# A hand-written step list that reaches from the start to the third batch's attention, in a kernel of cosine attention and a GELU feed-forward layer

## The chip, the cores and the metric

The kernel runs on one core of a Trainium2 chip. The metric is the device time of one execution in microseconds (us). TensorE does the matrix products, ScalarE the exponentials, the GELU and some squares, VectorE copies, sums and reciprocals, GpSimd the scaling of q and k and some squares and sums, and SyncE (SP) issues loads, stores and DMA transposes. GpSimd issues the loads that turn f32 into bf16. In the profile these engines are PE (and PEld for its weight loads), ACT, DVE, POOL and SP.

## The reference, cut to what matters

There are 8 batches, 12 heads, 448 positions and a head size of 64.

```python
q_n = q / (norm(q, axis=-1) + 1e-6);  k_n = k / (norm(k, axis=-1) + 1e-6)
scores = matmul(q_n, k_n.T) / tau                      # tau = 0.1
attn = exp(scores - max);  attn = attn / (sum(attn) + 1e-9)
x = matmul(attn, v)          # heads side by side: 3584 x 768
h = x @ w_in                 # 768 x 2048
g = 0.5 * h * (1 + erf(h / sqrt(2)))
out = g @ w_out              # 2048 x 768
```

## The kernel before

**Units of work.** Four heads of a batch make a quad g; a batch has three, so batch 0 has quads 0 to 2, batch 1 quads 3 to 5, batch 2 quads 6 to 8. The code also counts units u: quad 0 is cut into units 0 and 1, and from there unit u is quad u - 1. A quad's attention has these steps:

- `load_qk(g)` (L126) loads q and k through SP into one of four buffers, which is free again when the quad that held it has been scaled. `load_v` (L141), `load_wi` (L436) and `load_wo` (L445) are issued by POOL. `load_wo(0)` and `load_wo(1)` bring the upper and lower half of w_out's first 384 columns, `load_wo(2)` and `load_wo(3)` those of the last 384.
- `square`, `reduce`, `logs`, `roots`, `inverses`, `scale` (L151 to L208) give the normalised q and k in bf16: squares on ACT (L158) or POOL (L160), row sums on DVE (L168), Ln and Exp on ACT (L175, L180), the reciprocal on DVE (L188), the product on POOL (L204).
- `transposes` (L210) turns them, with TensorE and a DVE copy (`copies`, L226) up to unit 4, with a DMA on SP (L216) from unit 5.
- `scores` and `exps` (L232, L246) handle a quad in seven chunks: four matmuls into a pair of PSUM banks, then one Exp of 128x896 to SBUF. `visit(p)` (L654) does both for the next chunk in pair p. There are two pairs at first, and a third when batch 0's banks have been given up.
- The sum over keys is taken in three ways: `sums` (L298) with TensorE, `folded` (L258) with six POOL additions, `gathered` (L265) with DVE into PSUM. `turned` and `inverted`, or `turned_all` and `inverted_all` for the last two ways, bring the sums into place and invert them on DVE; `spread` (L362) lays them out.
- `values` (L324) multiplies by v, and `normalise` (L367) applies the inverse sum and writes x. It frees the banks that `values` filled.

**The feed-forward part.** x times w_in is the tile `hp` (`w_in`, L467): 16 column blocks m with six matmuls each. Each block is taken through GELU on ACT (L929). g times w_out is the tile `op` (`second_pieces`, L397): sixteen matmuls, called pieces, fill one of two banks, then a DVE copy (L410) empties it and SP stores it. Batch 0 gives 96 pieces and batch 1 128; the pieces are strewn between the scores of the next batch as filler for TensorE.

**What sets the order.** Each engine runs its instructions in the order of the program text, and each tile has a fixed buffer; an instruction waits for its data and for its buffer. Batch 0's attention is written out as a list (`attention_first`, L472). After it come `first(0)` (batch 0's hp), `attention(1)` (L702, pieces of batch 0, scores of batches 1 and 2), `first(1)`, `attention(2)`, `first(2)` and so on, each built by loops and counts such as

```python
        if b == 1:
            parts = iter((20, 13, 14, 17, 16, 16))
        elif b == 2:
            parts = iter((22, 12, 12, 13, 11, 13, 11, 11, 11, 6, 6))
```

which are the numbers of pieces between visits. `spin` (L460) issues idle matmuls. `total` (L371) for quads 3 to 7 uses `sums` on TensorE; quad 8 uses `folded`.

Of the kernel before, what the change touches and what calls it, by code (L numbers as in the profile page):

```python
# [9 lines left out]
F32 = mybir.dt.float32  # L10
# [6 lines left out]
def kernel(  # L17
# [108 lines left out]
    def load_qk(g):  # L126
        b, n = divmod(g, NQ)
        t = qkp.tile([128, 2, 2, C, D], F32, tag="qk", name=f"qk{g}")
        qk_t[g] = t
        for s0, s1 in ((0, 1), (1, 2)) if g == 0 else ((0, 2),):  # L130
            for i, src in enumerate((q, k)):
                eng = nc.scalar if g == 0 and s0 == 0 and i == 1 else nc.sync
# [131 lines left out]

    def gathered(g, p):  # L265
# [58 lines left out]
    def values(g, chunks=range(C), p=None):  # L324
        for c in chunks:
            if c == 0 and g < NQ:
# [70 lines left out]
    def second_pieces(sb, t, ni):  # L397
        state = {}

        def mm(kf):  # L400
# [8 lines left out]
            if kf == KF - 1:  # L409
                nc.vector.tensor_copy(ot[:, ni * NH:(ni + 1) * NH], ps[:, :NH])  # L410
# [7 lines left out]
        return [lambda kf=kf: mm(kf) for kf in range(KF)]  # L418
# [46 lines left out]
    early = {}  # L465

# [5 lines left out]
    def attention_first():  # L472
        x_t[0] = xp.tile([128, KD, S], BF16, tag="x", name="x0")
        DV, AC, GP = nc.vector, nc.scalar, nc.gpsimd
        Q, K = 0, 1
        square(0, ((AC, Q),))
        square(0, ((AC, K),))
        reduce(0, Q)
        reduce(0, K)
        square(1, ((AC, Q),))  # L480
        upto(load_v, 1)
        logs(0)
        reduce(1, Q)
        roots(0)
        upto(load_wi, 1)
        square(1, ((AC, K),))
        inverses(0)
        square(2, ((AC, Q),))
        reduce(1, K)
        scale(0, ((GP, 1),))  # L490
        logs(1)
        reduce(2, Q)
        roots(1)
        scale(0, ((GP, 0),))
        spin(2)
        transposes(0, 1)
        square(2, ((AC, K),))
        inverses(1)
        spin(1)
        transposes(0, 0)  # L500
        square(3, ((AC, Q),))
        copies(0, 1)
        scale(1, ((GP, 0),))
        copies(0, 0)
        square(3, ((AC, K),))
        scale(1, ((GP, 1),))
        upto(load_qk, 5)
        spin(1)
        transposes(1, 0)
        reduce(2, K)  # L510
        scores(0, ((0, 0), (0, 1)))
        upto(load_v, 2)
        transposes(1, 1)
        copies(1, 0)
        logs(2)
        scores(0, ((0, 2), (0, 3)))
        roots(2)
        upto(load_wi, 2)
        exps(0, ((0, 0), (0, 1)))
        inverses(2)  # L520
        copies(1, 1)
        exps(0, ((0, 2), (0, 3)))
        spin(2)
        scores(0, ((0, 4), (0, 5)))
        scale(2, ((GP, 0),))
        reduce(3, Q)
        exps(0, ((0, 4), (0, 5)))
        spin(1)
        scores(0, ((1, 0), (1, 1)))
        reduce(3, K)  # L530
        exps(0, ((1, 0), (1, 1)))
        spin(1)
        scores(0, ((1, 2), (1, 3)))
        scale(2, ((GP, 1),))
        upto(load_qk, 6)
        transposes(2, 0)
        exps(0, ((1, 2), (1, 3)))
        sums(0, (0,))
        copies(2, 0)
        scores(0, ((1, 4), (1, 5)))  # L540
        logs(3)
        scores(0, ((0, 6), (1, 6)))
        roots(3)
        transposes(2, 1)
        exps(0, ((1, 4), (1, 5)))
        inverses(3)
        sums(0, (1,))
        scale(3, ((GP, 0),))
        copies(2, 1)
        sums(0, (2,))  # L550
        exps(0, ((0, 6), (1, 6)))
        sums(0, range(3, 5))
        scores(1, ((0, 0), (1, 0)))
        scores(1, ((0, 1), (1, 1)))
        sums(0, (5,))
        exps(1, ((0, 0), (1, 0)))
        sums(0, (6,))
        upto(load_wi, 3)
        transposes(3, 0)
        turned(0)  # L560
        exps(1, ((0, 1), (1, 1)))
        scores(1, ((0, 2), (1, 2)))
        values(0, (0,))
        scale(3, ((GP, 1),))
        upto(load_wi, 4)
        copies(3, 0)
        values(0, (1,))
        exps(1, ((0, 2), (1, 2)))
        values(0, (2,))
        scores(1, ((0, 3), (1, 3)))  # L570
        inverted(0)
        values(0, range(3, 5))
        spread(0, 1)
        values(0, (5,))
        exps(1, ((0, 3), (1, 3)))
        scores(1, ((0, 4), (1, 4)))
        values(0, (6,))
        spread(0, 0)
        sums(1, (0,))
        square(4, ((GP, K),))  # L580
        exps(1, ((0, 4), (1, 4)))
        sums(1, (1,))
        scores(1, ((0, 5), (1, 5)))
        normalise(0, 0)
        transposes(3, 1)
        exps(1, ((0, 5), (1, 5)))
        scores(1, ((0, 6), (1, 6)))
        copies(3, 1)
        sums(1, (2,))
        square(4, ((GP, Q),))  # L590
        square(5)
        upto(load_wo, 2)
        exps(1, ((0, 6), (1, 6)))
        sums(1, range(3, 5))
        normalise(0, 1)
        scores(2, ((0, 0), (1, 0)))
        sums(1, (5,))
        exps(2, ((0, 0), (1, 0)))
        sums(1, (6,))
        scores(2, ((0, 1), (1, 1)))  # L600
        turned(1)
        values(1, range(2))
        exps(2, ((0, 1), (1, 1)))
        values(1, (2,))
        scores(2, ((0, 2), (1, 2)))
        inverted(1)
        values(1, range(3, 5))
        spread(1, 0)
        values(1, (5,))
        exps(2, ((0, 2), (1, 2)))  # L610
        values(1, (6,))
        scores(2, ((0, 3), (1, 3)))
        sums(2, (0,))
        reduce(4, K)
        normalise(1, 0)
        exps(2, ((0, 3), (1, 3)))
        sums(2, (1,))
        scores(2, ((0, 4), (1, 4)))
        spread(1, 1)
        values(2, (0,))  # L620
        sums(2, (2,))
        exps(2, ((0, 4), (1, 4)))
        scores(2, ((0, 5), (1, 5)))
        normalise(1, 1)
        values(2, range(1, 3))
        exps(2, ((0, 5), (1, 5)))
        values(2, (3,))
        scores(2, ((0, 6), (1, 6)))
        exps(2, ((0, 6), (1, 6)))
        reduce(4, Q)  # L630
        spin(1)
        early[4] = mm_tile("hp0_4")[:, :S]
        w_in(0, early[4], 4, range(2))
        sums(2, range(3, 7))
        values(2, (4,))
        logs(4)
        turned(2)
        values(2, (5,))
        roots(4)
        values(2, (6,))  # L640
        inverted(2)
        inverses(4)
        scale(4)
        spread(2, 1)
        spread(2, 0)
        normalise(2, 1)
        normalise(2, 0)
        done.update({square: 6, reduce: 5, root: 5, scale: 5, transposes: 5})

# [49 lines left out]

    def attention(b, fill):  # L702
        fill = list(fill)
        if b == 1:
            parts = iter((20, 13, 14, 17, 16, 16))
        elif b == 2:
            parts = iter((22, 12, 12, 13, 11, 13, 11, 11, 11, 6, 6))
        elif len(fill) == 128:
# [31 lines left out]
        if b == 1:  # L740
            upto(scale, u + 3)
            upto(load_v, b + 2)
            upto(transposes, u + 3)
            upto(load_qk, g0 + NQ + 2)
            upto(square, u + 4)
            visit(0, 1, 2)
            run()
            visit(0, 1, 2)
            run()
            upto(load_qk, g0 + NQ + 3)  # L750
            visit(0, 1)
            upto(square, u + 5)
            run()
            visit(0, 1, 2)
            both(g0, 0)
            upto(load_v, b + 3)
            upto(load_qk, g0 + NQ + 4)
            visit(1, 2)
            upto(reduce, u + 4)
            run()  # L760
            visit(1, 2, 0)
            both(g0 + 1, 1)
            visit(2, 0)
            logs(6)
            roots(6)
            run()
            both(g0 + 2, 2)
            inverses(6)
            done[root] = 7
        elif b == 2:  # L770
            upto(scale, u + 3)
            upto(load_qk, g0 + 6)
            upto(transposes, u + 3)
            upto(scale, u + 4)
            upto(load_qk, g0 + 7)
            upto(transposes, u + 4)
            visit(0, 1, 2)
            run()
            visit(0, 1, 2)
            norms(9)  # L780
# [230 lines left out]
```

## Time and profile before

| what | value |
|---|---|
| three runs | 400.55, 400.91, 400.94 us, median 400.91 |
| profiled execution, first to last instruction (span) | 398.6 us |
| around the span, median minus span | 2.3 us |
| busy PE, ACT, DVE, POOL | 392.0, 267.8, 264.0, 250.6 us |
| first hp matmuls of batch 0 that run on without a break | from 32.65 us |
| batch 0's hp ends, pieces and batch 1's scores begin | 51.33 us |
| batch 1's hp | 79.15 to 97.44 us |
| batch 2's hp begins | 133.45 us |

The page of the profile lists no separate device time for the profiled execution, so its own time is taken as its span and the 2.3 us around it. A row of the chain of waits has a start, a length in us, an engine, a tile and a line; x and a number count merged instructions. A row of a group has the line, engine, operation, result and operands, shapes, count, busy time in us, mean time of one in ns, and then the idle time ahead of it with what ended it. The profile counts a busy PE where matmuls overlap, so how full PE is is better read from the chain.

### The profile page before, as it was taken

To read this page: it belongs to the slowest core of one execution; us is meant where nothing else is said; L and a number is where in the kernel's file an instruction comes from. 1 tells how busy PE (TensorE), PEld (TensorE's weight loads), DVE (VectorE), ACT (ScalarE), POOL (GpSimd) and SP (SyncE) were. 2 spreads that over 40 slices of the span, in tenths; PEclk is the share of its full clock that TensorE was granted. 3 is DMA by queue.
4 is the path that set the end of the run, shared out by engine and by line. 5 is a ranking of instruction groups with operands and counts; after the bars stand their busy time and mean duration, and the time that the engine had idled before them with its cause. 6 is when DMAs were issued, how large, how long until landed. Compare 5 with 4: busy or idle time off the path is not lost.

```text
span 398.6 us, 8027 instructions
## 1 busy us (share of the span) xinstructions
PE 392.0 (98%) x3245; PEld 207.8 (52%) x3245; DVE 264.0 (66%) x530; ACT 267.8 (67%) x399; POOL 250.6 (63%) x162
## 2 busy tenths in 40 slices
PE   7999999999999999999999999999999999999996
PEld 3444555555545555555555555555555555555564
DVE  5787214955487999589963999769973797461021
ACT  6995787557988877888665977889656756504300
POOL 5898814269699694959587394969768391920000
PEclk9999999999999999999999999999999999999999
DMA  8999999747296890678145591566024720130033
GB/s 290 261 258 217 205 233 308 154 106 226 50 254 234 158 230 2 178 150 207 70 105 138 126 240 38 162 113 147 2 27 101 148 46 2 41 77 3 1 80 80
DMA packets 66485, 54.52 MB, mean 137 GB/s; under 512 B 38672, under 2 KB 62352, under 8 KB 66448
## 3 DMA queue, kind: packets, MB, share of 16 engines
q1 hardware_dynamic: 54464, 41.79, 39.0%
q0 software_dynamic: 11600, 11.80, 18.8%
q8 instruction: 25, 0.41, 0.4%
q10 hardware_dynamic: 384, 0.43, 0.3%
q14 instruction: 12, 0.10, 0.1%
HBM read 45.61 MB, written 11.01 MB: 142 GB/s over the span
## 4 chain that ended last, share of the span: by engine, by line
PE 95%; issue 1%; DVE 1%; POOL 1%; ACT 0%; POOLq 0%
PE hp L469 37%; PE op L406 36%; PE st L242 9%; PE o L320 4%; PE o L335 4%; PE op L425 1%; PE sm L305 1%; PE sh L667 1%; PE tp L221 1%; PE sm L314 1%; PE spin L463 0%; POOL wi L441 0%; DVE nq L168 0%; POOL qkb L204 0%; POOL v L145 0%
## 5 line engine op out<-in xcount | busy, mean ns | idle before, releaser
L252 ACT ACTIVATE pt<-st 128x896 bf16<-128x896 f32 x155 | 132.5, 916 | 29.0 <-PE st L242 28.4
L406 PE MATMUL op<-wo,g 128*128 128x384 bf16 x864 | 148.1, 326 | 0.0
L469 PE MATMUL hp<-x,wi 128*128 128x448 bf16 x768 | 147.0, 353 | 0.1
L204 POOL TENSOR_TENSOR qkb<-qk,rn 128x896 bf16<-128x896 f32 (+1 forms) x50 | 80.2, 1628 | 66.3 <-DVE rn L188 64.9
L406 PEld LDWEIGHTS <-g 128*128 128x128 bf16 x864 | 81.4, 98 | 62.6 <-issue 11.2
L469 PEld LDWEIGHTS <-wi 128*128 128x128 bf16 x768 | 74.4, 98 | 71.1 <-issue 2.8
L263 POOL TENSOR_TENSOR acc<-acc,pt 128x896 f32<-128x896 f32 x55 | 103.8, 1887 | 4.3
L929 ACT ACTIVATE g<-hp 128x448 bf16<-128x448 f32 x128 | 63.6, 552 | 63.6 <-PE hp L469 63.5
L410 DVE COPY ot<-op 128x384 f32<-128x384 f32 x54 | 29.9, 555 | 83.1 <-PE op L406 80.8
L168 DVE TENSOR_REDUCE nq<-sq 128x14 f32<-128x896 f32 (+1 forms) x50 | 50.6, 1038 | 10.2 <-POOL sq L160 6.7
L242 PE MATMUL st<-qkT 64*64 64x448 bf16 x620 | 46.0, 356 | 0.2 <-ACT pt L252 0.2
L160 POOL TENSOR_TENSOR sq<-qk 128x896 f32<-128x896 f32 x18 | 29.9, 1683 | 16.3 <-DMA qk<-in_q_dram 10.9
L369 DVE TENSOR_TENSOR x<-o,rs 128x448 bf16<-128x448 f32 x48 | 28.0, 609 | 9.9 <-PE sh L667 6.4
L270 DVE TENSOR_TENSOR acc<-acc,pt 128x896 f32<-128x896 f32 x30 | 33.0, 1099 | 1.0
L158 ACT ACTIVATE sq<-qk 128x896 f32<-128x896 f32 (+1 forms) x32 | 27.8, 902 | 2.2 <-DMA qk<-in_q_dram 1.8
L364 DVE STREAM_TRANSPOSE rs<-rc 128x448 f32<-128x448 f32 x48 | 28.7, 626 | 0.6
L242 PEld LDWEIGHTS <-qkT 64*64 64x64 bf16 x620 | 17.9, 105 | 20.5 <-issue 12.7
L263 POOL TENSOR_TENSOR acc<-pt 128x896 f32<-128x896 bf16 x11 | 20.7, 1879 | 8.9 <-DVE x L369 8.9
L320 PE MATMUL o<-pt,v 64*64 64x448 bf16 x364 | 24.2, 351 | 0.0
L673 ACT ACTIVATE pt<-sh 128x448 bf16<-128x448 f32 x26 | 14.1, 544 | 9.2 <-PE sh L667 8.5
L276 DVE STREAM_TRANSPOSE ta<-acc 128x448 f32<-128x448 f32 x32 | 18.5, 617 | 0.2
L335 PE MATMUL o<-pt,v 64*64 64x448 bf16 x308 | 17.5, 351 | 0.5 <-DVE x L369 0.5
(54 smaller groups left out, 212.4 us busy)
## 6 DMA issues: line engine op xcount, KB each, us to landing
qk<-in_q_dram SPq DMA_DIRECT2D x23, 448.0 KB, 4.6
qk<-in_k_dram SPq DMA_DIRECT2D x23, 448.0 KB, 5.4
out_dram<-ot SPq DMA_DIRECT2D x48, 192.0 KB, 3.2
v<-in_v_dram POOLq DMA_DIRECT2D x7, 672.0 KB, 7.7
wo<-in_moe_w_out_dram POOLq DMA_DIRECT2D x4, 768.0 KB, 11.6
wi<-in_moe_w_in_dram POOLq DMA_DIRECT2D x4, 512.0 KB, 14.4
out_dram<-ot SPq DMA_DIRECT2D x12, 96.0 KB, 2.1
wi<-in_moe_w_in_dram POOLq DMA_DIRECT2D x4, 256.0 KB, 14.6
```

Source lines behind the costliest of these rows:

```text
L160: eng.tensor_tensor(sq, t, t, ALU.mult)
L168: nc.vector.tensor_reduce(nq_t[n][:, j, i], sq_t[g, i][:, s0:s1], mybir.AxisListType.X, ALU.add)
L204: eng.tensor_tensor(qkb[:, i, :, s0:s1].rearrange("p c s d -> p s c d"), t[:, i, s0:s1], rn[:, i].to_broadcast([128, s1 - s0, C, D]), ALU. ...
L242: nc.tensor.matmul(st[cols, n, :S], lhsT=qkT[rows, 1, c, cols], rhs=qkT[rows, 0, :, cols], start=True, stop=True, tile_position=(64 * s, 6 ...
L252: nc.scalar.activation(pt, st[:, :, :S], AF.Exp, scale=inv_tau)
L263: nc.gpsimd.tensor_tensor(acc_t[g], all_t[g][:, 0] if c == 1 else acc_t[g], all_t[g][:, c], ALU.add)
L270: nc.vector.tensor_tensor(acc_t[g], acc_t[g], all_t[g][:, c], ALU.add)
L320: nc.tensor.matmul(bank_t[g, h][64 * s:64 * (s + 1), :S], lhsT=v_t[g][rows, s, c, :], rhs=pt_t[g, s, c][rows], start=(c == 0), stop=(c == ...
L335: nc.tensor.matmul(bank_t[g, h][cols, :S], lhsT=v_t[g][rows, s, c, :], rhs=pt_t[g, s, c][rows], start=(c == 0), stop=(c == C - 1), tile_po ...
L406: nc.tensor.matmul(ps[:, :NH], lhsT=g_t[sb][:, kf, t * 128:(t + 1) * 128], rhs=wo[:, kf, ni * NH:(ni + 1) * NH], start=(kf == 0), stop=(kf ...
L469: nc.tensor.matmul(t, lhsT=wi[:, kd, m * 128:(m + 1) * 128], rhs=x_t[b][:, kd, :], start=(kd == 0), stop=(kd == KD - 1))
L929: nc.scalar.activation(g_t[sb][:, m, hf * S:(hf + 1) * S], hps.pop(m), AF.Gelu)
```

## The change

`attention_first`, `first(0)`, `attention(1)`, `first(1)` and `attention(2)` are taken out. A new function, `opening`, is a list of 581 steps that does their work, and only the steps of the first loads stay as they were. `first(2)` and all behind it keep their code. The helpers that the list needs are new: `run(n, eng)` issues n pieces, `bank`, `banks`, `mm` and `gelu` issue the parts of hp one at a time, `more(b)` makes batch b's pieces available. The pieces' copies may now be put on ACT: `run(1, AC)` does so for eight of the fourteen tiles. `gather` is new too: it sums quad 3, the first of batch 1 (the second batch), on DVE into an SBUF buffer of the squares' tag, where `sums(3)` on TensorE did it. Quads 4 to 7 keep `sums`, quad 8 keeps `folded`.

The order of each engine's queue changes. POOL's, from the start: `load_v(0)`, `load_v(1)`, scale 0 Q, scale 0 K, scale 1 Q, `load_wi(0)`, scale 1 K, square 3 K, scale 2 K and Q, `load_wi(1)`, scale 3 Q and K, `load_wi(2)`, square 4 Q, `load_wi(3)`, square 6 K, scale 4 Q and K, `load_wo(0)`, square 6 Q, square 7 Q, `load_wo(1)`, square 7 K, `load_wo(2)`, scale 5 Q, scale 6 Q, scale 5 K, scale 6 K, `load_wo(3)`, `load_v(2)`. The numbers are units. SP loads quad 5 before quad 4, and quad 6 earlier than it did. ACT no longer does square 3 K but square 4 K. The parts of the diff that matter here:

```diff
+    def gather(g, c):
+        if c == 1:
+            acc_t[g] = sqp.tile([128, 2, S], F32, tag="sq", name=f"acd{g}")
+        nc.vector.tensor_tensor(acc_t[g], all_t[g][:, 0] if c == 1 else acc_t[g], all_t[g][:, c], ALU.add)
+
...
-                nc.vector.tensor_copy(ot[:, ni * NH:(ni + 1) * NH], ps[:, :NH])
+                (nc.scalar.copy if eng is nc.scalar else nc.vector.tensor_copy)(ot[:, ni * NH:(ni + 1) * NH], ps[:, :NH])
...
+    def run(n, eng=nc.vector):
+        for _ in range(n):
+            todo_t.pop(0)(eng)
+
+    def banks(b, m, p):
+        st = pair(p, f"hp{b}_{m}")
+        hps_t[b, m], hps_t[b, m + 1] = st[:, 0, :S], st[:, 1, :S]
+
+    def mm(b, m, k0, k1):
+        w_in(b, hps_t[b, m], m, range(k0, k1))
...
+    def opening():
...
+        scale(1, ((GP, 0),))
...
+        load_wi(0)
+        scores(0, ((0, 2), (0, 3)))
+        reduce(2, K)
+        scores(0, ((0, 0), (0, 1)))
+        square(3, ((AC, Q),))
+        transposes(1, 0)
+        spin(1)
+        reduce(2, Q)
+        scale(1, ((GP, 1),))
+        transposes(1, 1)
+        exps(0, ((0, 2), (0, 3)))
+        scores(0, ((0, 4), (0, 5)))
+        exps(0, ((0, 0), (0, 1)))
+        spin(1)
+        copies(1, 0)
+        square(3, ((GP, K),))
+        logs(2)
...
+        scores(2, ((0, 6), (1, 6)))
+        exps(2, ((0, 6), (1, 6)))
+        logs(4)
+        roots(4)
+        table(GELU_SET)
+        banks(0, 0, 1)
+        banks(0, 2, 0)
+        values(2, (2,))
+        values(2, (3,))
+        values(2, (4,))
+        inverses(4)
+        scale(4, ((GP, Q),))
+        values(2, (5,))
+        sums(2, (3,))
+        sums(2, (4,))
+        sums(2, (5,))
+        sums(2, (6,))
+        turned(2)
+        inverted(2)
+        values(2, (6,))
+        bank(0, 4)
+        mm(0, 4, 0, 2)
+        scale(4, ((GP, K),))
+        mm(0, 1, 0, 4)
...
+        run(7)
+        gather(3, 1)
+        load_qk(7)
+        square(8, ((AC, Q),))
+        scale(6, ((GP, Q),))
+        run(6)
+        scale(5, ((GP, K),))
+        run(1)
+        reduce(7, K)
+        visit(0)
+        visit(1)
+        gather(3, 2)
+        visit(2)
+        run(6)
+        gather(3, 3)
+        gather(3, 4)
+        run(9)
+        visit(0)
+        transposes(5)
+        gather(3, 5)
+        gather(3, 6)
+        turned_all(3)
+        inverted_all(3)
+        scale(6, ((GP, K),))
+        transposes(6)
+        visit(1)
+        load_wo(3)
+        visit(2)
+        spread(3, 1)
+        run(8)
+        run(1, AC)
+        load_v(2)
+        run(1)
...
+        visit(1)
+        values(3, p=0)
+        visit(2)
+        visit(1)
+        normalise(3, 0)
+        load_v(4)
+        sums(4)
+        visit(2)
+        x_t[2] = xp.tile([128, KD, S], BF16, tag="x", name="x2")
+        visit(0)
+        normalise(3, 1)
...
-        if b == 1:
-            upto(scale, u + 3)
...
-            both(g0, 0)
...
+    opening()
+    assert not todo_t, len(todo_t)
+    first(2)
+    for b in range(3, B):
+        attention(b, output_pieces(b - 1))
+        first(b)
```

The count of matmuls, exponentials, GELUs, spins (29) and table loads (nine up to batch 2's hp) is the same on both sides, apart from the 16 matmuls of `sums(3)` and, on DVE, the operations of quad 3's sum. `load_qk` has a new argument that no call uses.

More of the change, by code (lines that the diff above doesn't have):

```diff
@@ L470, in w_in @@
                              start=(kd == 0), stop=(kd == KD - 1))
[L472 to L648, printed above, removed]
@@ new lines, in attention @@
+        upto(scale, u + 5)
+        upto(transposes, u + 5)
+        upto(load_qk, g0 + 9)
+        mixed(g0, 0, (1,), (2, 1))
+        squared(u + 6, 0)
+        folded(g0 + 2, range(3))
+        run()
+        for h in range(2):
+            spread(g0 + 1, h)
+        if b + 1 < B:
+            visit(2, 0, 1)
+        else:
+            visit(2, 0)
+            weighted(g0 + 1, 1)
+            visit(2)
+        folded(g0 + 2, range(3, 6))
+        run()
+        for i in range(2):
+            reduced(u + 5, i)
@@ L861, in attention @@
+        if b + 1 < B:
+            mixed(g0 + 1, 2, (0,), (1, 0))
+        squared(u + 6, 1)
+        folded(g0 + 2, range(6, 7))
+        upto(load_v, b + 3)
+        run()
+        reduced(u + 6, 0)
+        visit(1, 2, 0)
+        run()
+        reduced(u + 6, 1)
+        visit(1, 2, 0)
+        norms(2 * b + 6)
+        turned_all(g0 + 2)
+        run()
+        inverted_norms(2 * b + 6)
+        inverted_all(g0 + 2)
+        mixed(g0 + 2, 1, (2,), (0, 2), True)
         assert not fill, len(fill)
@@ L868, in first @@
         u = (b + 1) * NQ + 1
[L869 to L871 removed]
+        hps = {}
+        pairs = ({2: 2, 4: 1, 8: 2}, {2: 0, 4: 2, 8: 0})[min(b, 3) - 2]
+        ahead = 6
         def mm(m, kds):
@@ L920, in first @@
         for m in range(KF):
-            if b == 0 and m == 8:
-                for i in range(2):
-                    transposes(4, i)
-                    copies(4, i)
             if m >= ahead and (m == 0 or m - 1 not in pairs):
@@ L972, with more, open_third @@
         fill = [f for t, ni in todo if t not in tail for f in second_pieces(sb, t, ni)]
-        fill += [f for t in tail for f in last_pieces(sb, t)]
-    for f in fill:
+        return fill + [f for t in tail for f in last_pieces(sb, t)]
+    def more(b):
+        todo_t.extend(output_pieces(b))
+    def open_third():
+        acc.close()
+        third.append(ctx.enter_context(tc.tile_pool(name="ps_third", bufs=1, space=bass.MemoryType.PSUM)))
+    opening()
[4 more added lines that the diff above has]
+        first(b)
+    for f in output_pieces(B - 1):
         f()
```

700 lines of the change are left out of this document (523 added, 177 removed).

## The prediction

> **What bounds the kernel.** I first read the engines' busy shares and the slices on the page, then the chain that ended last.
>
> ```profile
> PE 392.0 (98%) x3245; PEld 207.8 (52%) x3245; DVE 264.0 (66%) x530; ACT 267.8 (67%) x399; POOL 250.6 (63%) x162
> ...
> PE   7999999999999999999999999999999999999996
> ...
> PE 95%; issue 1%; DVE 1%; POOL 1%; ACT 0%; POOLq 0%
> ```
>
> TensorE is the bound in every slice but the first, and the chain runs on it for 95%. A new order of the same work can therefore gain only where the chain leaves PE, or by taking work off PE. The chain in order of time shows where. Up to 8.65 it waits for loads and POOL; then it leaves PE twice:
>
> ```profile
> 10.17 0.62 DVE qkT L226
> 10.79 1.00 DVE nq L168
> 11.81 0.33 ACT lq L175
> 12.16 0.23 ACT root L180
> 12.39 0.81 ACT pt L252
> ...
> 25.19 0.66 DVE tr L343
> 25.87 0.34 DVE rc L360
> 26.23 0.65 DVE rs L364
> 26.94 0.83 issue
> 27.77 0.62 DVE x L369
> ```
>
> These are about 3.1 us and 3.2 us. From 28.43 to 389.93 the chain is PE without a hole, batch 1's stage included:
>
> ```profile
> 64.85 0.69 PE st L242 x12
> 65.54 0.78 PE sm L314 x16
> 66.32 1.45 PE o L335 x28
> 67.77 0.42 PE st L242 x8
> 68.18 2.71 PE op L406 x16
> ```
>
> So everything after 32.65, where hp runs on, is a sum of PE work. Any wait that the new list lets in there costs its full length. The groups between 8 and 32.7, shapes apart, say what holds the start:
>
> ```profile
> L252 ACT ACTIVATE pt<-st 128x896 bf16<-128x896 f32 x21 | 17.8, 915 | 0.8 <-PE st L242 0.7
> ```
>
> Between the first Exp (12.29, from the timeline) and the last one's end (29.49 + 1.73 = 31.22), 18.9 us, ACT is busy with 21 Exps and two small pairs of Ln and Exp. The start is bound by ACT with PE close behind.
>
> **Quad 3's sum leaves PE.** The 16 sm matmuls of one quad are one row of 0.78, on the chain. They go: -0.78. Their place is not filled.
>
> **Changes of tile shape.** In the chain, 4, 8 and 12 score matmuls take 0.31, 0.50 and 0.69: 0.19 a chunk and 0.12 for the change of shape; pieces go the same way (11 in 1.90, 13 in 2.22). I counted such blocks from 51.33 to 133.45: 45 in the chain, 43 in the list. 2 x 0.12: -0.25.
>
> **The start.** I walked the new queues by hand with durations of the timeline.
> - To 5.60 nothing changes. POOL then issues both v pieces (0.89 + 0.83) and starts scaling at 7.3 (before: 7.62). Three scalings of 0.91 end at 10.05; `load_wi(0)` (1.22) stands ahead of the fourth, which ends at 12.2 (before: 7.62 + 3.64 = 11.26).
> - The first scores need both copies, 10.37, so the first Exp starts at 11.0, 1.3 earlier.
> - Quad 1 comes later than this: square 3 K (1.67, now on POOL, its buffer free at 12.45), two scalings to 17.45, transposes 0.56, copy 0.62, score: its first Exp can start at 19.1. Before it was 18.66.
> - Until then ACT has seven Exps at 0.81 (5.7), two Ln and Exp pairs (1.2) and square 4 K (0.95): 18.8, and 19.15 with a wait of 0.35 for row sums. Both threads meet there.
> - Fourteen Exps follow. With two pairs of banks two Exps take 1.71 in the timeline (19.47 to 21.18), 0.855 each: 12.0, so the last ends at 31.2, as before.
> - Behind the last Exp PE has one chunk of sums and one of values, 0.31 each, so hp starts at 31.9. Before it runs on at 32.65 with 0.37 of hp done, so at 32.28. That is -0.4.
>
> The bounds: were ACT never waiting after 11.0, then 21 x 0.81 + 1.2 + 0.95 + 0.1 gives 30.25, hp at 30.9, -1.4. If waits like those before (18.66 to 31.22 is 0.6 over 14 x 0.855) return, +0.2, and twice that +0.8. I take -0.3, nearest to the walk.
>
> **Batch 1's stage.** DVE sums quad 3 with six additions, and the trace has DVE's addition only with the accumulator in PSUM:
>
> ```profile
> L270 DVE TENSOR_TENSOR acc<-acc,pt 128x896 f32<-128x896 f32 x30 | 33.0, 1099 | 1.0
> ```
>
> Both operands now lie in SBUF. POOL does that form in 1.89 (L263), so I bound it by 0.6 (an x operation of half the size) and 1.89 and take 1.1. Six are 6.6, with the two transposes (1.17), the row sums and reciprocal (2.8) some 10.6, against 3.2 for `turned`, `inverted` and their like. DVE is busy 14.55 of 27.80 there, so the room exists. The order decides: the first addition is behind a piece copy at 55.9, the chain with a row sum and one piece copy in it ends `spread(3, 0)` at 69.0, and after a row sum (1.04) and two `normalise` (0.6 each) at 71.2. The visit of chunk 4 of quad 5 needs that bank; PE gets there at 70.9. I add +0.3 (from 0 to +1.0). The piece copies between the additions come at most 0.4 us before their bank is wanted.
>
> **What I cost at nothing, and its cover.** The transfers: wi's second part, issued at 17.7 (before 12.02), lands by the packets' pace at about 30 and is wanted at 32.6; its last at 36 to 38, wanted at 41.5. The pieces' copies on ACT: I take 0.5 (half Exps, 128x448, take 0.544; the DVE copy 0.555). Three stand in batch 1's stage, where ACT is busy 21.38 of 27.8. The squares moved between POOL and ACT keep their sum. DMA transposes of units 5 and 6 follow scalings that end at 50.7 and 52.4; wanted at 60 and 68, and they took 3.4 to 12.3 to land.
>
> **The sum.** -0.78 - 0.25 - 0.3 + 0.3 = -1.03. The span becomes 397.6, and with the 2.3 around it, which this does not touch, 399.9. The profiled execution's span and the median of 400.91 differ by that 2.3. A change under 0.2%, 0.8 us, is about what the measurement can't tell from none: 400.1 to 401.7.
>
> **Rivals.**
> 1. *The early Exp is kept whole.* For it: 1.3 us at the first Exp. Against: quad 1's scaling at 17.45. -0.78 - 0.25 - 1.4 = 398.5.
> 2. *ACT becomes the bound in batch 2's attention.* Before:
>
> ```profile
> 97.40:133.40 36.00, 36.00 (x386) 18.51 (x386) 24.15 (x53) 33.18 (x44) 27.86 (x18) 1.00 0.71 180
> ```
>
> The fourth busy figure is ACT's, 33.18 of 36.00. Five copies come (2.5), a square goes (0.95): 34.7. Its waits for scores there were some 2.2; if they stay, it needs 36.9, 1.0 more than the stage has. 400.9, as before the change.
> 3. *Slower: the last part of w_out comes late.* `load_wo(3)` was issued at 41 and now stands behind `load_wo(2)` and four scalings. Square 7 Q waits for a buffer until 40.6; then two squares, two issues and four scalings (1.65 each) put it at 52.4. The row
>
> ```profile
> wo<-in_moe_w_out_dram POOLq DMA_DIRECT2D x4, 768.0 KB, 11.6
> ```
>
> has the median landing; the four lay between 8.5 and 13.8. Piece 57 wants it at 63.6: the point is 11.2 after the issue. At 13.8 PE waits 2.6, and all behind it: 399.9 + 2.6 = 402.5. Each us by which POOL is later adds one. Against: less other traffic then than in those rows.
> 4. *The additions and POOL hold each other up.* No row has DVE reading two SBUF tiles beside a working POOL. By my walk POOL has nothing to compute from 52.4 to 73. If its scalings ran 5 us late, three additions would each wait for one, 3 x 1.65; DVE's chain would end near 76.2, and PE wait 5.3: 404.9. The Trainium skill, SBUF — State Buffer, section "SBUF: two separate sides", states such a rule: a VectorE operation with two SBUF inputs and a GpSimd operation that reads SBUF exclude each other for a whole instruction. No row of this trace shows it; by it alone, with POOL idle as I have it, the forecast stays.
>
> That the change does not do what it says is not a case of its own: the matmuls do go.
>
> **Chances.** Forecast 0.44 (399.2 to 400.7; 0.30 of it under 400.1, 0.14 within), first rival 0.12, second 0.16 (0.14 within, 0.02 slower), third 0.22 (0.02 within, 0.20 slower), fourth 0.06. Faster 0.42, same 0.30, slower 0.28. Range 398.6 to 402.8: below it lies half of the first rival, above it the fourth and a part of the third.
>
> **What would show it.** No sm row between quad 3's scores and its values, and 0.78 less PE work from the first hp to batch 2's hp. First Exp at 11.0, quad 1's first at 19.1, hp from 31.9. Batch 2's hp would start at 132.4 (before: 133.45). A hole in PE at a visit near 71, with DVE `normalise` as its end, is the +0.3; a hole before a piece near 63.6 ended by a DMA of wo is the third rival; visits that wait for ACT between 98 and 132 are the second. I would be wrong if PE stood still for more than 1 us anywhere after 32, or if the stages behind 133 changed length, which I hold to be the same.

## The result and the profile after

The changed kernel takes 403.44 us (403.03 to 404.08, 6 runs) beside 400.90 for the kernel before: a ratio of 1.0068, 95% interval 1.0056 to 1.0079. I had forecast 399.9, in a range up to 402.8. It is slower, and outside the range. The profiled execution took 404.08, its span is 402.3. Some executions were disturbed; the ratios and the time of e3 leave them out, and the profile of e3 is of such a one.

The page of the changed kernel, busy shares, PE's slices and the chain:

```profile
PE 390.9 (97%) x3229; PEld 207.8 (52%) x3229; DVE 269.1 (67%) x533; ACT 274.1 (68%) x412; POOL 242.2 (60%) x157
...
PE   7997998999998999999999999999999999999996
...
PE 79%; DMA 10%; POOL 5%; issue 2%; ACT 2%; DVE 1%; SPq 0%; POOLq 0%; DVEq 0%
```

PE has 1.1 us less to do, but three slices behind the start are no longer full, and the chain leaves PE for 21% of the span, half of that to transfers. PE's waits between 30 and 137 us (columns: total, times, longest) say which:

```profile
PE st L242 <- DMA qkT<-qkb: 2.6, 2, 1.6
PE hp L472 <- DVE x L374: 2.0, 1, 2.0
PE st L242 <- DVE x L374: 0.2, 1, 0.2
```

The chain in order of time (start, length, what) shows how the 2.0 comes about:

```profile
12.57 16.85 DMA qk<-in_k_dram
...
29.55 1.68 POOL sq L160
...
31.26 1.09 DVE nq L168
32.35 0.56 DVE rs L369
...
33.00 0.64 DVE x L374
...
33.68 2.43 PE hp L472 x12
```

Quad 5's keys are issued at 12.57 and land 16.85 later. POOL's square of them (square 6 K) waits for them; VectorE's row sum of that square stands, in the list, ahead of quad 1's last spread and `normalise`; and the bank that hp's block 4 wants is free only behind that. PE had nothing to do from 31.67 to 33.68.

The same view, at batch 1's stage:

```profile
48.98 3.30 POOL qkb L204 x2
52.28 0.67 SPq L216
...
53.12 16.93 DMA qkT<-qkb
...
70.09 0.38 PE st L242 x4
```

The DMA transposes of quad 5 (unit 6), wanted at 68.5, land at 70.1, 16.9 us after their issue at 53.12. Those of quad 4 (unit 5), issued at 50.66, landed in 6.3 us, and nobody waited for them. Before, the same visit ran without a hole (64.85 to 70.9 in the lines shown there). The third wait, 1.07 up to 129.41, is the same for quad 10: its transposes were ready from 115.8, but on SP's queue they stood behind two stores that waited for a piece copy until 118.62 and behind quad 14's loads, and were issued at 121.72.

From batch 2's hp on nothing differs: it starts at 137.21 and 265.1 us follow, against 133.45 and 265.15 before. So the account is made between hp and hp (columns: stretch, length, PE busy, matmuls, clock, DMA share, GB/s); first the kernel before, then the changed one:

```profile
32.28:133.45 101.17, 101.17 (x909) 1.00 0.87 194
```

```profile
33.68:137.21 103.53, 100.63 (x887) 1.00 0.92 190
```

The start ends 0.6 earlier (31.67 against 32.28), the first hole costs 2.0, the waits behind it 2.8, and PE's work shrank by 0.5. Together +3.7, and the 3.76 by which batch 2's hp is later.

### The profile page after: what moved, and what is told of

Its sections match the earlier page's. It is cut to its first block, busy times and chain, and to the rows that moved or that the text cites. A ratio compares the mean times of both kernels' runs of the same rounds, so it can differ in the third digit from the quotient of the medians.

```text
span 402.3 us, 8020 instructions
## 1 busy us (share of the span) xinstructions
PE 390.9 (97%) x3229; PEld 207.8 (52%) x3229; DVE 269.1 (67%) x533; ACT 274.1 (68%) x412; POOL 242.2 (60%) x157
## 4 chain that ended last, share of the span: by engine, by line
PE 79%; DMA 10%; POOL 5%; issue 2%; ACT 2%; DVE 1%; SPq 0%; POOLq 0%; DVEq 0%
PE hp L472 33%; PE op L411 31%; DMA qkT<-qkb 6%; PE st L242 6%; PE o L325 4%; DMA qk<-in_k_dram 4%; POOL qkb L204 3%; PE o L340 2%; PE op L430 1%; PE sh L518 1%; POOL acc L263 1%; ACT pt L252 1%; ACT g L501 1%; POOL sq L160 0%; POOL v L145 0%
## 5 line engine op out<-in xcount | busy, mean ns | idle before, releaser
L411 PE MATMUL op<-wo,g 128*128 128x384 bf16 x864 | 149.7, 326 | 0.0
L415 DVE COPY ot<-op 128x384 f32<-128x384 f32 x46 | 25.5, 555 | 71.1 <-PE op L411 68.9
L160 POOL TENSOR_TENSOR sq<-qk 128x896 f32<-128x896 f32 x13 | 21.8, 1684 | 29.9 <-DMA qk<-in_k_dram 26.0
L158 ACT ACTIVATE sq<-qk 128x896 f32<-128x896 f32 (+1 forms) x37 | 32.4, 908 | 7.0 <-DVE nq L168 3.3
L325 PE MATMUL o<-pt,v 64*64 64x448 bf16 x364 | 24.2, 351 | 0.0
## 6 DMA issues: line engine op xcount, KB each, us to landing
wi<-in_moe_w_in_dram POOLq DMA_DIRECT2D x4, 256.0 KB, 10.5
```

Of the source, the lines that this page charges most:

```text
L158: eng.activation(sq, t, AF.Square)
L325: nc.tensor.matmul(bank_t[g, h][64 * s:64 * (s + 1), :S], lhsT=v_t[g][rows, s, c, :], rhs=pt_t[g, s, c][rows], start=(c == 0), stop=(c == ...
L411: nc.tensor.matmul(ps[:, :NH], lhsT=g_t[sb][:, kf, t * 128:(t + 1) * 128], rhs=wo[:, kf, ni * NH:(ni + 1) * NH], start=(kf == 0), stop=(kf ...
```

## The experiments

All ratios are to the kernel before, measured beside each on the same chip (its medians: 400.66 to 400.89).

### One cause at a time: e1, e2, e3, and together: e4

e1 moves one row sum behind the `normalise` that PE waits for.

```
-        reduce(6, K)
         sums(2, (0,))
...
         normalise(2, 0)
+        reduce(6, K)
         mm(0, 3, 0, 4)
```

> One edit on the changed kernel: the row sum of unit 6's k (DVE) stands behind quad 2's normalise and no longer ahead of quad 1's second spread and normalise. Theory (three separate waits for transfers): the 2.0 us hole of PE at 31.7 goes, hp starts at 31.7 in place of 33.7. The wait for quad 5's DMA transpose stays and may grow by what PE comes earlier, up to 2 us, since the transpose lands by the traffic and not by PE. So 401.4 if that transpose moves with the rest, 403.4 if it does not. Rival (hp waits for w_in or for the Exps as well): hp starts at 33 or later and nothing changes, 403.4, with another releaser in the hole.

402.67 us, 1.0058 (1.0037 to 1.0078). PE's waits from 20 to 140 us:

```profile
PE st L242 <- DMA qkT<-qkb: 2.5, 2, 1.7
PE st L242 <- DVE x L374: 0.2, 1, 0.2
```

The hole ahead of hp is gone (hp starts at 31.58), and the other waits stayed; the transposes now are the next thing late. So the row sum's place was its cause. The profiled execution, at 401.69 the fastest of the seven, is 2.4 under the changed kernel's; the median fell by only 0.8, and the intervals of the two ratios overlap, so that the gain in time is seen in the trace alone.

e2 takes batch 3's values out of POOL's queue beside the transposes.

```
         normalise(3, 0)
-        load_v(4)
...
         scale(7, ((GP, K),))
+        load_v(4)
```

> One edit on the changed kernel: the load of v for quads 9 to 11 is issued some 29 us later, behind the scaling of unit 7. Theory (POOL's queue of packets shares the DMA engines packet by packet with the transposes): quad 5's transpose lands before 68 in place of 70.1, the 1.6 us hole at 68.5 goes, 401.9. Rival (the transpose is late because its scaling was late or because a transpose of this size takes its 17 us): it lands at 70 as before, 403.4.

403.7 us, 1.0076 (1.0059 to 1.0093): no gain. Yet the wait for quad 5's transposes fell from 1.6 to 0.2. In its place PE waited 0.6 for VectorE's `normalise` near 72, the end of quad 3's sum, which the later hole had covered, and 0.8 near 128 for Exps that stood behind a piece copy on ScalarE. A hole removed gave the time to the next one behind it.

e3 issues quad 10's transposes right after `sums(7)`, ahead of the store.

```
         sums(7)
+        transposes(11)
         folded(8, (1,))
...
         folded(8, (4,))
-        transposes(11)
```

> One edit on the changed kernel: quad 10's DMA transpose stands on SP ahead of the stores and of quad 14's load, right behind quad 9's. Theory (it is late by its place on SP): issued by 118 in place of 121.7, it lands by 126, the hole of 1.1 us at 128.3 goes, 402.4. Rival (its scaling, or a buffer of the transposed tiles, holds it): issue stays near 121 and the time at 403.4.

403.26 us, 1.0058 (1.0043 to 1.0072): no gain that stands clear of the changed kernel's interval. The third wait is gone from its profile. e4 shows the same.

e4 is e1, e2 and e3 together.

> The three edits together. Theory: the holes are the whole loss, 2.0 + 1.6 + 1.1 = 4.7 us, so 398.8, faster than the kernel before by 0.5%. Rival (a hole closed opens another behind it, since all wait for the same full DMA engines): 400 to 402, with a new releaser on PE.

401.03 us, 1.0010 (0.9998 to 1.0023). The three reorderings take back what the change had lost, and bring the kernel to the time of the one before, not below: the rival's outcome. 0.8 of waiting for quad 5's transposes is left and 0.5 for the last part of w_out.

### Is it that the DMA engines are full? e5, e7, e9, e10

My theory at this point: POOL's queue is nearly empty from 36 to 40 us, since `load_wo(0)` now is issued at 37.56 (before: 30.01), and w_out's 3 MB push everything behind them. e7 is the changed kernel with w_out's parts early; e5 is e4 with the same and with the scalings of units 5 and 6 ahead of unit 7's squares. The edit of e7 (the four later calls go):

```
+        load_wo(0)
+        load_wo(1)
         square(6, ((GP, K),))
...
+        load_wo(2)
         square(6, ((GP, Q),))
...
+        load_wo(3)
         square(7, ((GP, Q),))
```

> The three edits of before, and on POOL the four loads of w_out earlier (two in its idle time ahead of square 6 K, near 26 and 27, one ahead of and one behind square 6 Q) and the scalings of units 5 and 6 ahead of the squares of unit 7. Theory (the transposes of quads 4 and 5 are slow because w_out's packets take turns with theirs): w_out has landed by 53, the second transpose lands by 60, no hole of PE between 31.7 and batch 2's hp but some 0.5 on DVE, batch 2's hp at 132.3 to 132.8 (before 133.45), the time 399.6 to 400.2. Rival (loads and transposes only change places in full DMA engines): another wait on a load appears on PE, and the time stays at 401.

> The changed kernel with the four loads of w_out earlier on POOL, and nothing else. Theory: the wait of 1.6 for quad 5's transpose goes, the waits at 31.7 (2.0) and at 128 (1.1) stay: 401.9. Rival (v's two loads slow the transpose, not w_out's): the transpose lands near 70 and the time stays at 403.4.

Both failed badly: e5 406.54 us, 1.0136 (1.0106 to 1.0167); e7 410.5, 1.0239 (1.0221 to 1.0257). By 52 us the early order had moved no more than the late one (6.95 MB from 24 us on in e5, 7.06 in e4): from 36 to 40 us the engines move 346 GB/s in e4, where quad 7's load has them almost alone, and 270 in e5, where it shares them with w_out's small packets. PE waits 3.4 (e5) and 5.9 us (e7) for transposes, and these are not quad 5's but quad 4's, for which nobody waited in the changed kernel. In e5 they are issued at 47.86 and land 15.3 later, when quad 4's first chunk has long been wanted:

```profile
63.19 0.96 PE L242 MATMUL st<-qkT 64*64 64x448 bf16 x8 [3.38 <-DMA qkT<-qkb]
```

The packets from 54 to 56 us say why (columns: packets, MB, share of 16 engines). q0 is POOL's queue (w_out, values), q1 is SP's (here the transposes). First the changed kernel, then e5:

```profile
q1 hardware_dynamic: 1304, 0.33, 98.5%
q0 software_dynamic: 23, 0.01, 4.8%
```

```profile
q0 software_dynamic: 375, 0.28, 90.7%
q1 hardware_dynamic: 374, 0.10, 37.7%
```

In the changed kernel w_out's last part is issued late, at 52.23, and so leaves a gap in POOL's queue through which quad 4's transposes pass. With all of w_out issued early that gap is filled.

The long wait costs a second time. e5 and then e7 by stretches of 2 us (columns: stretch, length, then busy time and count of PE, PEld, DVE, ACT, POOL, then PE's granted clock, DMA share, GB/s):

```profile
60.00:62.00 2.00, 0.00 (x0) 0.00 (x0) 1.96 (x3) 0.79 (x1) 0.00 (x0) 0.94 1.40 80
```

```profile
62.00:64.00 2.00, 0.00 (x0) 0.00 (x0) 1.90 (x4) 0.85 (x1) 0.00 (x0) 1.00 1.61 102
64.00:66.00 2.00, 0.00 (x0) 0.00 (x0) 1.86 (x3) 0.00 (x0) 0.00 (x0) 0.70 1.39 110
66.00:68.00 2.00, 0.17 (x4) 0.17 (x8) 1.97 (x3) 0.00 (x0) 0.00 (x0) 0.50 1.43 170
68.00:70.00 2.00, 2.00 (x13) 0.62 (x10) 1.80 (x10) 1.53 (x2) 0.00 (x0) 0.50 1.43 96
...
72.00:74.00 2.00, 2.00 (x18) 1.00 (x12) 0.29 (x1) 1.99 (x4) 0.00 (x0) 1.00 1.26 147
```

In e7 PE idles from 61.9 to 67.8, the clock falls to half within 64 to 66, and it is back only near 72. From the first hp to the end PE is busy for 364.2 us, against 362.2 in the changed kernel: 1.9 more for the same matmuls (in e5 2.6 more than in e4).

e9 takes 0.92 MB from in front of w_out and the transposes: quad 7's load goes behind them on SP's queue.

```
-        load_qk(7)
-        square(8, ((AC, Q),))
...
         transposes(6)
+        load_qk(7)
...
+        square(8, ((AC, Q),))
         square(8, ((AC, K),))
```

> On top of the three reorderings of e4 (401.0 us, 0.8 us of waiting for quad 5's transpose and 0.5 for a part of w_out left): the queries and keys of quad 7 (0.92 MB) are loaded behind quad 5's transposes on SP's queue, where the changed kernel loads them at 37.6, and their squares and row sums come as much later. My theory, that the 16 DMA engines are full from 5 to 65 us so that whatever is issued ahead of the transposes moves them: w_out and then the transposes land 3 to 4 us earlier, both waits go, 399.5 to 400.1. Rival, that small transpose packets are slow beside any packet of w_out or v, whatever the total: the transposes land as before, 400.8 to 401.3.

401.57 us, 1.0022 (1.0004 to 1.0041). Quad 5's transposes landed 16.4 us after their issue, about as in e4 (16.3), and the wait of 0.8 stayed; w_out's 0.5 went, and 0.4 for VectorE's copy of a piece, behind quad 7's moved row sum, came. The theory of full engines falls: 0.92 MB less ahead of the transposes did not move them, and from 52 to 54 us, beside them, the engines were busy to a share of only 0.45, at 68 GB/s.

e10 adds w_out's first two parts early.

> As e9, and the first two parts of w_out issued ahead of the squares of quad 5's keys (near 27 us, as the kernel before did near 30). My theory: with quad 7's load gone from 36 to 44 the early parts fill the engines that would otherwise run with POOL's queue empty, w_out ends 2 us earlier still, but no wait is left to be shortened: within 0.2 us of e9. Rival, that early w_out slows quad 5's key load, as a hole ahead of batch 0's w_in: 0.5 to 1.5 us over e9, with hp from 32.5 or later.

401.51 us, 1.0020 (1.0005 to 1.0036). Here the wait for the transposes is gone; PE waits 0.2 for values and the same 0.4 for the copy. Other than in e5, w_out's last part is still issued late here (51.27), and both transposes are faster: quad 4's landed in 3.7 us and quad 5's in 10.5.

### Packet by packet: e12, e13

The packets of the two queues also say why quad 5's transposes crawl. The changed kernel between 58 and 66 us (columns as above; then the issue and its landing):

```profile
q0 software_dynamic: 1221, 1.01, 92.2%
q1 hardware_dynamic: 1191, 0.30, 40.6%
...
qkT<-qkb SPq DMA_TRANSPOSE x1, 16.9
```

Each queue gets about as many packets through as the other, 1221 and 1191, though the transposes' have only 256 B. So a transpose's some 1800 packets (0.46 MB) wait for as many of POOL's, and w_out's last part and the values have about that many (1538 in POOL's queue from 56 to 68 us in e9). The Trainium skill, DMA: Bandwidth & Descriptors, section "Queues, rings and completion order", says that each DMA engine goes round its queues packet by packet; the equal counts agree, though that the page and the profile count the same thing as a packet is not shown.

e12 keeps POOL's queue clear: e10, with w_out's last part ahead of the four scalings and the values behind a one-element copy that waits for the transposed tile (and a row sum moved).

```
         load_wo(2)
+        load_wo(3)
...
-        load_wo(3)
...
+        touch(5)
         load_v(2)
```

> As e10 (first two parts of w_out early, quad 7's load behind quad 5's transposes), and POOL's queue kept clear beside the transposes: the last part of w_out is issued ahead of the four scalings, and batch 1's values behind a one-element copy that waits for quad 5's transposed tile; quad 7's query row sum also stands behind a copy that PE waited 0.4 us for. My theory now, that a 256 B packet of a transpose gets one turn for each packet of POOL's queue, whatever the total: with no packet there quad 5's transpose lands within 6 to 10 us of its issue (16.4 in e9), by 62; the values land by 68.5, no wait over 0.3 us is left between 32 and 134, 399.0 to 400.0. Rival, that transposes are slow by themselves at this place: they land at 66 to 68 as before, the values, issued behind them, at 71 or later, and PE waits 2 us or more for values: 402 or more.

e12 from 56 to 58 us:

```profile
q1 hardware_dynamic: 2049, 0.53, 125.4%
...
qkT<-qkb SPq DMA_TRANSPOSE x1, 5.8
```

2049 packets in 2 us with POOL's queue empty, where it was about 300 in 2 us beside it. Quad 4's transposes land 7.1 us after their issue and quad 5's 5.8, by 58.5. This is the theory's number, and the rival's (landing at 66 to 68) is out. PE's waits from 28 to 140 us:

```profile
PE hp L472 <- DVE ot L415: 0.5, 1, 0.5
PE st L242 <- DVE x L374: 0.2, 1, 0.2
```

No transfer is left among them. But the time is 401.23 us, 1.0015 (0.9994 to 1.0036): no faster than e4, and over what I expected. In the two profiles the stretch from hp to batch 2's hp is 0.4 shorter than in e4 (101.66 against 102.09), but hp starts 0.8 later (32.81 against 31.98); the reason for that is under "Open" below.

e13 clears POOL's queue in the same way in e4, with quad 7's load and the first parts of w_out where the change has them.

> e4 (401.0) with only POOL's queue kept clear beside quad 5's transposes: last part of w_out ahead of the four scalings, batch 1's values behind a copy that waits for the transposed tile; quad 7's load and the first parts of w_out stay where the changed kernel has them. My theory: w_out's rest still runs beside the first transpose, so quad 5's lands by 64 to 65, its 0.8 us of waiting goes, w_out's 0.5 goes with the earlier issue, the values land near 70 and cost 0 to 1.5: 399.7 to 401.2. Rival (transposes slow by themselves): 402 or more.

403.32 us, 1.0065 (1.0041 to 1.0088): the rival's time, without the rival's reason. Quad 5's transposes were issued some 3 us later than in e4 (55.06), took 8.7 us, landed at 63.8, even before the 64 to 65 of the theory, and their wait is gone. Quad 4's, beside which w_out's last part now ran, took 10.6 in place of 8.1, and PE waited 0.8 for them; the values, issued behind at 64.06, cost 2.0. The mechanism held; the sum was wrong.

### Is there a gain under the waits? e14, e15

e14 is e12 with the last 0.5 taken away: the piece's copy ahead of two row sums, a square of ScalarE behind three Gelus.

```
-        reduce(8, K)
         run(1)
+        reduce(8, K)
         reduce(8, Q)
...
-        square(10, ((AC, Q),))
         gelu(1, 2)
...
         gelu(1, 5)
+        square(10, ((AC, Q),))
```

> e12 (401.23 against 400.85 of the kernel before) with the last wait of batch 1's w_in taken away: VectorE copies the piece of the second GEMM ahead of two row sums of quad 7 and ScalarE squares quad 8's queries behind three Gelus. If 1.0 us of TensorE work is really saved, as I had worked out, and only waits had hidden it, no wait over 0.3 us being left, the kernel is now below the one before: 0.3 to 0.6 under e12, 400.6 to 400.9. If the saving is only the 0.5 of the changed kernel's trace, it is the same as before within 0.2%: 400.8 to 401.3.

401.37 us, 1.0012 (0.9996 to 1.0028), close to the second of the two outcomes. PE's work from hp to batch 2's hp is 100.9, 0.3 under the kernel before; 0.5 of waiting for two Gelus took the place of the copy.

e15 is e14 with w_out's first parts late again (35.7 and 40.1).

> e14 with the first two parts of w_out back where the changed kernel issues them (35.7 and 40.4 us). POOL's queue is clear beside the transposes all the same, but w_out ends later: if only POOL's queue beside the transposes counts, quad 5's land 1 to 2 us later than in e14 and still in time, 0 to 0.3 from e14; if w_out's start counts as well, a wait of 0.5 or more for w_out or the transposes comes back and it is 0.5 to 1.0 over e14.

404.47 us, 1.0051 (1.0018 to 1.0084). The executions spread from 401.67 to 405.13, and the profiled one, at 402.33, is among the fastest; why the others took longer is not shown. In it the values wait 1.8, since the transposes they follow land later: w_out's start counts as well, the second of the two outcomes.

### Quad 3's sum by itself: e6, e8, e11

e6 puts the sum on VectorE into the kernel before, and nothing else of the change.

```
             visit(0, 1, 2)
+            for c in range(1, 3):
+                gather(g0, c)
             run()
...
+            gather(g0, 6)
+            turned_all(g0)
+            inverted_all(g0)
...
-            both(g0, 0)
+            weighted(g0, 0)
```

> The kernel before with one part of the change alone: quad 3 is summed on DVE by additions into an SBUF tile between the visits, its sums on TensorE go. Theory (a row of 0.78 leaves PE and DVE has the time): batch 2's hp starts 0.8 earlier, 399.9. Rival (DVE's longer work delays the copies of the pieces or quad 3's normalise): 400.7 or more, with DVE as the releaser of a PE wait between 60 and 75.

402.78 us, 1.0057 (1.0037 to 1.0076): slower. PE waits 2.3 for a piece's copy, which stands on VectorE behind the additions, and the additions are longer than in the changed kernel. VectorE and POOL in order of time, from short windows of the timeline (start, length, engine, line), and the spread of the five additions (ns, shortest, median, longest):

```profile
58.09 1.67 POOL L160 TENSOR_TENSOR sq<-qk 128x896 f32<-128x896 f32 x1 [7.76 <-DMA qk<-in_q_dram]
58.65 2.06 DVE L268 TENSOR_TENSOR acd<-acd,pt 128x896 f32<-128x896 f32 x1
60.63 1.68 POOL L160 TENSOR_TENSOR sq<-qk 128x896 f32<-128x896 f32 x1 [0.87 <-DMA qk<-in_k_dram]
60.81 2.44 DVE L268 TENSOR_TENSOR acd<-acd,pt 128x896 f32<-128x896 f32 x1
```

```profile
L268 DVE TENSOR_TENSOR acd<-acd,pt x5: 1092/1093/2443, 56.3 to 64.6; 128x896 f32<-128x896 f32 x5
```

Three additions take 1.09. The two that begin while POOL squares take 2.06 and 2.44, and both end 0.9 to 1.0 after POOL's square does: nearly all their work comes once POOL is done. Together they are 2.3 us longer than two of 1.09; VectorE works without a gap from the first of them to the piece copy, and PE's wait for that copy is 2.3. This is my fourth rival's mechanism, in the kernel where POOL is not idle. The rule of the Trainium skill, SBUF — State Buffer, section "SBUF: two separate sides", that the two exclude each other for a whole instruction, is borne out by these rows. In the changed kernel POOL computes nothing between 52.3 and 75, and the additions run at 1.09 throughout:

```profile
L268 DVE TENSOR_TENSOR acd<-acd,pt 128x896 f32<-128x896 f32 x5 | 5.4, 1088 | 0.3
```

e8 and e11 go the other way: sm matmuls back on TensorE, in e5 and in e9.

```
-        gather(3, 1)
...
+        sums(3)
+        turned(3)
+        inverted(3)
         values(3, p=0)
```

> As the first kernel of this call, but quad 3's sum is back on TensorE with DVE's short chain, ahead of its values. Theory: 0.78 of PE comes back, less what PE waited for DVE there (0 to 0.6): 0.2 to 0.8 above the first kernel. Rival: DVE's additions cost PE more than they save, and this is the faster of the two.

> As e9, but quad 3's exponentials are summed by the 16 sm matmuls on TensorE again, right ahead of its values, and VectorE's six additions are gone. By the terms on record (0.78 of sm matmuls, part of the 0.25 of shape changes) 0.8 to 1.0 us over e9. Rival, that the additions cost VectorE as much as they spare TensorE, since the second GEMM's copies stand behind them: within 0.3 us of e9, or faster.

e8 408.18 us, 1.6 over e5; e11 404.23, 1.0083 (1.0067 to 1.0100), 2.7 over e9. PE's stretch from hp to batch 2's hp, e9 and then e11:

```profile
32.10:134.60 102.50, 100.87 (x889) 1.00 0.98 196
```

```profile
32.44:136.98 104.54, 101.75 (x903) 1.00 0.92 192
```

The matmuls are worth 0.88 of PE's time. The rest is waiting: 1.6 for VectorE's `normalise` (0.2 in e9) and 0.6 for ScalarE, less the 0.8 for transposes. So inside this list the sum on VectorE is a gain of 1.6 to 2.7 us, of which 0.9 is TensorE's work. The rest depends on where e8 and e11 put the sum, right ahead of the visits that need the bank; another place was not tried. In the kernel before it is a loss of 2.1, about as large as the 2.3 by which POOL stretched the additions.

## Why the prediction was wrong

**The transfers that I costed at nothing** are the step that failed. In place of nothing the runs showed three waits of TensorE for them: 2.0 us ahead of hp, 1.6 for quad 5's transposes and 1.07 for quad 10's. I wrote that the transposes of units 5 and 6 "follow scalings that end at 50.7 and 52.4; wanted at 60 and 68, and they took 3.4 to 12.3 to land". The scalings ended as walked, the last at 52.28. Quad 4's transposes landed within that range, in 6.3 us; quad 5's, issued at 53.12, took 16.9. The range of 3.4 to 12.3 came from rows beside which POOL's queue was nearly empty while most of the packets ran (48 of its packets from 52 to 54 us, 7 from 60 to 64). I had moved w_out from 30 to 37.6 us and two loads of values next to the transposes, and did not ask what those rows owed to their neighbours. Quad 10's transposes I did not place on SP's queue at all.

**The start.** The walk of engines was right: first Exp at 11.03 (11.0), quad 1's first at 19.41 (19.1), the last Exp's end 30.86 (31.2), PE free at 31.67 (31.9). Two errors cancelled in it: quad 1's first Exp came 0.3 later than walked, and the fourteen Exps behind it took 11.45 where I had 12.0. The rows:

```profile
11.03 1.73 ACT L252 ACTIVATE pt<-st 128x896 bf16<-128x896 f32 x2
...
19.41 11.45 ACT L252 ACTIVATE pt<-st 128x896 bf16<-128x896 f32 x14 [0.19 <-PE st L242]
```

But "hp starts at 31.9" needed a bank that a row sum held up, and the row sum needed quad 5's keys. I had walked wi and not this load. That hole is 2.0 of the 4.7 by which the profiled span, 402.3, passes the forecast's 397.6, and e1 removes it with one line.

**Quad 3's sum, -0.78,** is right (0.88 from e9 and e11), and so is the size of an addition (1.09 for 1.1). **The changes of shape, -0.25,** did not appear: PE's work fell by 0.5, not by 1.03, in e14 by 0.3. The count was wrong. From the end of batch 0's hp to the start of batch 2's, PE's rows in the timeline change shape 51 times before and 52 times in the changed kernel (hp and pieces taken as one shape), where I had 45 and 43 blocks. At my 0.12 each that is 0.12 more and not 0.25 less: 101.17 - 0.78 + 0.12 = 100.51, against 100.63 measured.

**The wait on `normalise`, +0.3,** is not in the changed kernel, since the later transposes cover it; e2 shows it, at 0.6. A piece's copy on ACT takes 0.51, as taken.

**The rivals.** The second did not occur in the changed kernel (PE waits for no Exp there), only in e2. Of the third, w_out's last part was issued at 52.23 (52.4) and landed in time; it shows as 0.5 in e4. The fourth's mechanism exists but had no POOL work to meet. The sentence that decided was the last: PE stood still for more than 1 us three times after 32. I had set it as what would prove me wrong and priced none of the three.

**The time around the span.** I added 2.3, a median less the span of one profiled execution. In every execution on record that has both, the two are 1.7 to 1.9 apart; so 0.5 of the 2.3 was the difference between two executions, and the forecast 0.5 too high by it.

**Open** is why the queues slow down for a while: from 60 to 68 us in e5 and 58 to 66 in e7 both were busy and moved only 80 to 110 GB/s. The changed kernel has such a stretch too, of 2 us (64 to 66, 103 GB/s), and e4 as well (62 to 64, 93 GB/s).

The lists of e1, e4, e9, e13 and e15 agree up to hp, and yet it starts between 31.6 and 32.6 in them, and in e12 at 32.81. This the traces show. All begin with 22 idle matmuls (`spin`). First the changed kernel, then e12, from the timeline:

```profile
1.95 5.81 PE L468 MATMUL spin<-g,ident 128*128 128x448 bf16 x22 [1.95 <-DVE root L92]
8.23 0.58 PE L221 MATMUL tp<-ident,qkb 128*64 128x128 bf16 x7 [0.47 <-POOL qkb L204]
```

```profile
1.95 7.39 PE L468 MATMUL spin<-g,ident 128*128 128x448 bf16 x22 [1.95 <-DVE root L92]
9.40 0.55 PE L221 MATMUL tp<-ident,qkb 128*64 128x128 bf16 x7
```

The idle matmuls start 0.37 us apart at first and 0.19 apart from some moment on: 4.6 us in the changed kernel's profile, 7.8 in e12's. In e12 they end so late that the first transposes on TensorE wait for them and no longer for POOL. The first Exp comes at 12.17 in place of 11.03, and hp starts 20.6 us behind the first Exp in e1, e4, e9, e12, e13, e14 and e15 alike. So where hp starts hangs on a moment that differs from execution to execution. The kernel before has the same idle matmuls; in its one profile they end at 8.30, and its transposes wait for POOL. Fewer idle matmuls at that place were not tried, and how much of the spread of the times comes from this is not shown.

No version here beats the kernel before; e4, e12 and e14 equal it.

## What to carry to other kernels

When a list of steps is written anew, walk the transfers with the same care as the engines: for each, its issue, what else is in the other queue at that time, and who stands in order behind the instruction that waits for it. Small-packet transfers such as transposes should be issued when the other queue is empty, and large loads behind them; a landing time read from a row holds only for that row's neighbours. In a kernel that one engine bounds, removing a hole gives its time to the next one, so undo causes together before judging them one by one.

## What the runs showed of the hardware

- The two queues got about the same number of packets through when both were full (1221 and 1191 in 8 us), whatever the packets' size. The DMA transposes of a quad, 1800 packets of 256 B, landed in 3.7 to 6.3 us where POOL's queue was empty or nearly so (quad 4's in e10 and in the changed kernel, quad 5's in e12), and in 16 to 17 beside w_out and values (quad 5's in the changed kernel, e1, e4 and e9).
- Where PE stood idle for 3.4 (e5), 4.2 (e8) and 5.95 us (e7), its granted clock fell to 0.50, and stayed there for about 4 to 5 us of work, which cost 1.9 (e7) and 2.6 us (e5); idle times of 2.3 (e6) and 2.0 us (e13) left it at 1.00. The Trainium skill, TensorE: Matmul & The Clock Gate, section "Part 1: The HAM clock gate (the "warmup" mystery)", has a window of about 3.4 us and a half rate for an idle array. The half rate agrees with these rows. A whole window of idleness was not needed in e5: 0.94 over 60 to 62 us is a half rate from 61.8 on, 2 us after PE had stopped at 59.8. So no length of a wait that is safe can be read from these rows.
- An addition on VectorE with two SBUF inputs takes 1.09 us alone and 2.06 to 2.44 if it begins while POOL squares.
